# A flag mask taken through DRAM instead of a matrix product, three stores made whole, and another pace for the scans

## The chip, the cores and the metric

The kernel runs on one core of a Trainium2 chip. The metric is the device time of one execution in microseconds (us). The engines are called as the profile calls them: PE (matrix products; PEld is its weight load), DVE (vector), ACT (scalar), POOL (GpSimd) and SP, which here does little but issue DMA transfers.

## The reference

The input `x` is 2048 tokens of 448 channels, float32. Two branches read it, and a gate per token mixes them:

```python
g = sigmoid((x * gate_w).sum(-1, keepdims=True))
# a: a state-space layer: a kernel K of 256 complex exponentials per channel, convolved along the tokens
K = 2.0 * einsum("dn,dnl->dl", C, exp((A * dt) * pos)).real
a = causal_convolution(K, x) + x * D_skip
# b: an MLP mixer
h  = gelu(layernorm(x) @ w1)            # 448 -> 448
x1 = x + shifted_by_group(h) @ w2       # four channel groups moved by +1, -1, +2, -2 tokens
b  = x1 + gelu(layernorm(x1) @ w3) @ w4 # 448 -> 1792 -> 448
out = g * a + (1 - g) * b
```

## The kernel before

**Units.** The tokens are cut into four blocks of 512, each of four tiles of 128. PE works through 72 units: 16 small ones of kind "a" (layer w1/w2, four per block), then 14 of kind "d" for each block (128 of the 1792 hidden channels each). One unit is a run of products `first` (line 478, 11 matmuls of 512 columns for a "d" unit) into a bank `p`, and two units later a run `second` (line 602, 12 matmuls of 448 columns) that adds into four banks `acc`, one for each tile. Every float32 operand is split into a high and a low part, so that three products stand for one. Between the two, ACT makes the gelu `uf` (line 539) and its high part `uh` (line 549), and DVE the low part `ul` (line 569). At the end of a block, DVE takes the four `acc` banks into the result tile `xs` (`residual`, line 615); the next block's first `second` overwrites those banks, and so waits for it.

**The state-space branch.** For small rates the long convolution is the sum of four running sums. `ssm_guard` computes their coefficients `nuf`, and a flag for each partition, `rk[:, 4]`, which is 1 where the rates are small enough. `ssm_mask` makes one answer of the 128 flags, in every partition: `okm`. Where it holds, the coefficients are copied into `nu`, which had been zero; where it doesn't, a general convolution runs behind the kernel (`tc.If` in `gated_mix_kernel`, line 59 and 60), and each engine reads `okm` for that. The input of a step is loaded with 1 MB into `zs` (`ssm_load`), scaled on ACT by `nu` (`ssm_scale`, line 752), run through four scans on DVE (`ssm_scan`, line 757, a carry going by POOL), summed (`ssm_sum`), transposed (`ssm_turn`), sent through DRAM (`yd`, `ysb`) and added to the result (`ssm_out`, line 787). There are 16 such steps.

**Order.** Nothing is scheduled by a tool. Each engine carries out its instructions in the order in which the Python code issues them. The loop over units `n` calls what `at(n, ...)` has entered in the lists `before`, `after`, `between` and `late`; the scans' queue is paced by `ssm_some`, which gives it a credit of so many us of DVE work for each unit. SP's transfers stand in one queue in the same order, and a transfer that has to wait holds up those behind it.

**Transfers and their eight counters.** Each transfer counts on one of eight semaphores, handed out in turn (DMAHW0 to DMAHW7, called lanes here). At the end of the program SP waits for lane 0, lane 1 and so on to lane 7, one instruction each (line 60). A tile of the result goes out when both its branches have been added (`done`): whole, but in two halves of 64 rows for the first block.

Of the kernel before, what the change touches and what calls it, by code (L numbers as in the profile page):

```python
# [8 lines left out]
F32 = mybir.dt.float32  # L9
# [3 lines left out]
OP = mybir.AluOpType  # L13
AX = mybir.AxisListType
# [14 lines left out]
NF = F // 128  # L29
# [150 lines left out]
def mixer_and_small_steps(ctx, tc, xs, gg, okm, x, xT, xb, x0, w1, w2, w3, w4, gate, par, logdt, dskip, ident, out):  # L180
    nc = tc.nc

    big = ctx.enter_context(tc.tile_pool(name="big", bufs=1))
    wk = ctx.enter_context(tc.tile_pool(name="wk", bufs=2))
    ps = ctx.enter_context(tc.tile_pool(name="ps", bufs=2, space=PSUM))
    dr = ctx.enter_context(tc.tile_pool(name="dr", bufs=1, space=bass.MemoryType.DRAM))
# [19 lines left out]
    one = big.tile([128, 1], F32, name="one")  # L206
# [3 lines left out]
    rk = big.tile([128, 8], F32, name="rk")  # L210
# [244 lines left out]
    units = [("a", b, g) for b in range(NB) for g in (0, 2, 1, 3)] + \  # L455
# [5 lines left out]
    def first(n, bank="p1", seq=None, stop=True):  # L461

        kind, b, i = units[n]
        xh, xl = XH[kind, b], XL[kind, b]
        if kind == "a":
            wh, wl = (w1d, None) if i == 2 else (w1h[:, TI[i]], w1l[:, TI[i]])
            o = HALO - SHIFT[i]
        else:
            wh, wl = (w[:, :, i * 128:(i + 1) * 128] for w in (w3h, w3l))
            o = 0  # L470
        fresh = n not in P1
        if fresh:
            P1[n] = ps.tile([128, TB], F32, name="p1", tag=bank, bufs=3 if bank == "p1" else 1)
        p = P1[n]
        every = [(w, x_, k, 0, TB) for x_, ks in ((0, (0, 1, 2)), (0, (3,)), (1, (0, 1, 2))) for w in range(2 - x_)
                 for k in ks if not w or wl is not None]
        for q, (w, x_, k, t0, t1) in enumerate(seq or every):
            nc.tensor.matmul(p[:, t0:t1], (wl if w else wh)[:, k, :], (xl if x_ else xh)[:, k, o + t0:o + t1],  # L478
                             start=(q == 0 and fresh), stop=stop if q + 1 == len(seq or every) else False)
# [5 lines left out]
    def act_add(n, part=None):  # L485
        p = P1[n]
        if not part:
            UF[n] = wk.tile([128, TB], F32, name="uf")
            nc.scalar.activation(UF[n][:GD], p[GD:], AF.Copy)
        if part is not False:  # L490
            nc.vector.tensor_add(UF[n][:GD], p[:GD], UF[n][:GD])
# [63 lines left out]
    def act_head(n, later=False):  # L555
        drain(head_ops(n))
        if not later:
            drain(copy_ops(n))

    def act_copy(n):  # L560
        drain(copy_ops(n))

    def act_tail(n):
        kind, b, i = units[n]
        uf = UF.pop(n)
        if kind == "a" and i == 2:
            nc.vector.tensor_sub(UH[n][GD:], uf[:GD], f32(UH[n])[:GD])
        else:
            nc.vector.tensor_sub(UL[n], uf, f32(UH[n]))  # L569
# [3 lines left out]
    def done(b, j):  # L573
        q = NT * b + j
        parts[q] = parts.get(q, 0) + 1
        if parts[q] == 2:
            for p in range(0, 128, 64 if b == 0 else 128):
                t = slice(p, p + (64 if b == 0 else 128))
                nc.sync.dma_start(out[q * 128 + t.start:q * 128 + t.stop], xs[t, q, :])

    ADDED = {}
# [1 line left out]
    def second(n, only=None):  # L583
        kind, b, i = units[n]
        if kind == "a":
            wh, wl = w2h[:, i, :], w2l[:, i, :]
            s, e = i == 0, i == 3
        else:
            wh, wl = W4[i]
            s, e = i == 0, i == NF - 1  # L590
        q = [(j, p) for p in range(2 if kind == "a" and i == 2 else 3) for j in range(NT)]
        if s or e:
            q.sort()
        for j, p in only or q:
            first_, last_ = s and p == 0, (e or n == len(units) - 3 and j == NT - 1) and p == 2
            if only:
                ADDED[j] = ADDED.get(j, 0) + 1
                first_, last_ = ADDED[j] == 1, ADDED[j] == 11
            if first_:
                ACC[j] = ps.tile([128, D], F32, name=f"acc{j}", tag=f"acc{j}", bufs=1)  # L600
            t = slice(j * 128, (j + 1) * 128)
            nc.tensor.matmul(ACC[j], (UL if p == 2 else UH)[n][:, t], wl if p == 1 else wh,  # L602
                             start=first_, stop=last_)
        if e and not only:
            for j in range(NT):
                residual(n, j)

    def residual(n, j):
        kind, b, i = units[n]
        q = NT * b + j  # L610
        r = xs[:, q, :]
        if kind == "a":
            nc.vector.tensor_add(r, ACC[j], r)
        else:
            nc.vector.scalar_tensor_tensor(r, ACC[j], gs[:, q:q + 1], r, op0=OP.mult, op1=OP.add)
            done(b, j)
# [104 lines left out]
    def ssm_guard():  # L721
# [7 lines left out]
        nc.vector.tensor_scalar(rk[:, 0:4], rk[:, 0:4], RHO / L, None, op0=OP.is_le)  # L729
        nc.vector.tensor_reduce(rk[:, 4:5], rk[:, 0:4], axis=AX.X, op=OP.min)  # L730

    def ssm_mask():
        p = ps.tile([128, 1], F32, name="misc", bufs=1)
        nc.tensor.matmul(p, one.to_broadcast([128, 128]), rk[:, 4:5], start=True, stop=True)  # L734
        nc.vector.tensor_copy(rk[:, 5:6], p)
        nc.vector.tensor_scalar(okm, rk[:, 5:6].to_broadcast([128, 16]), 127.5, None, op0=OP.is_ge)
        nc.vector.copy_predicated(nu.rearrange("p a b -> p (a b)"), okm, nuf.rearrange("p a b -> p (a b)"))

    ZZ, ZS = {}, {}
# [66 lines left out]
    def ssm_some(n, amount):  # L806
        credit[0] += amount
        while queue and credit[0] > 0.0:
            cost, fn, a = queue.pop(0)
            credit[0] -= cost  # L810
            fn(*a)
            if fn is ssm_turn and a[1] == 3:
                for i in range(NT):
                    at(n + 1 + i // 2, ssm_back, a[0], i, when=late)
                    at(n + (2 if a[0] + 1 == NB else 3) + i // 2, ssm_out, a[0], i, when=late)
# [3 lines left out]
    before, between, after, late = {}, {}, {}, {}  # L819

    def at(n, fn, *a, when=after):
        when.setdefault(n, []).append((fn, a))

    def run(when, n):
        for fn, a in when.pop(n, []):
            fn(*a)
# [291 lines left out]
    def begin():  # L1118
        constants()
        first_loads()  # L1120
        nc.scalar.activation(rt, cm[:, 0:1], AF.Gelu_apprx_tanh)
        hl_tiles(("a", 0))
        hl_tiles(("a", 1))
        warm_up(7)
        for word in ORDER.split():
            name, _, codes = word.partition(":")
            if name[0] == "p" and codes:
                products(int(name[1]), codes)
            elif codes:
                second(int(name[1]), [(int(c[0]), int(c[1])) for c in codes.split(",")])  # L1130
            else:
                next(TASKS[name])
# [51 lines left out]
    for b in range(NB):  # L1184
        s0 = (7, 18, 31, 46)[b]
        for i in range(NT):
            n = s0 + (3, 4, 5, 3)[b] * (i // 2)
# [4 lines left out]
            q, when = n + (4 if b in (1, 2) else 3), late if b == 3 else before  # L1192
# [11 lines left out]
        for m in range(4):  # L1204
            at(q[m], ssm_moment, k, m)
    at(33, ssm_guard)
    at(34, ssm_mask, when=between)
    at(33, ssm_queue)
    for m in (3, 2, 1, 0):
        at(OWN, ssm_scale, 0, 0, m)  # L1210

# [2 lines left out]
    with tc.manual_schedule():  # L1214
        begin()
        for n in range(4, len(units)):
            if n >= 4 * NB - 2 and n + 1 < len(units):
                act_tail(n + 1)
            run(before, n)
            spent = sum(cost.get(fn, 0.0) for when in (after, late) for fn, _ in when.get(n, []))  # L1220
            run(after, n)
            if n < 4 * NB - 2 and n not in (7, 11):
                act_tail(n + 1)
            if n + LAG < len(units):
                first(n + LAG)
                if units[n + LAG][::2] == ("a", 2):
                    act_add(n + LAG, False)
            if n in (7, 11):
                second(n)
                act_tail(n + 1)  # L1230
            if n + LAG in UF:
                act_add(n + LAG, True)
            if n < OWN:
                run(between, n)
            if n + LAG < len(units) and n not in (6, 10):
                act_head(n + LAG, True)
            run(between, n)
            if n + LAG < len(units) and n not in (6, 10):
                act_copy(n + LAG)
            if n >= OWN:  # L1240
                ssm_some(n, 3.75 - (2.2 if units[n][2] == NF - 1 else 0.0) - spent)
            run(late, n)
            if n < len(units) - 2 and n not in (7, 11):
                second(n)
        last_two()
# [55 lines left out]
```

## Time and profile before

| what | before |
|---|---|
| median of 3 runs | 371.3 us (371.2 to 372.18) |
| the profiled execution | 371.42 us, span 369.6 us, granted clock 0.997 |
| PE busy | 363.9 us (98%) |
| DVE busy | 308.5 us (83%) |
| ACT busy | 216.1 us (58%) |
| POOL busy | 63.8 us (17%) |
| chain that ended last | PE 95%, DMA 3% |

The profiled execution took 371.42 us, of which 369.6 us lie between the first and the last instruction in the trace; a time worked out on the trace is set against 371.42, which is 0.1 us over the median. In the rows of the timeline the columns are: start in us, length in us, engine, line, operation, out<-in, count, and in brackets how long the engine stood idle before and what ended that.

### The profile page before, as it was taken

To read this page: it belongs to the slowest core of one execution; us is meant where nothing else is said; L and a number is where in the kernel's file an instruction comes from. 1 tells how busy PE (TensorE), PEld (TensorE's weight loads), DVE (VectorE), ACT (ScalarE), POOL (GpSimd) and SP (SyncE) were. 2 spreads that over 40 slices of the span, in tenths; PEclk is the share of its full clock that TensorE was granted. 3 is DMA by queue.
4 is the path that set the end of the run, shared out by engine and by line. 5 is a ranking of instruction groups with operands and counts; after the bars stand their busy time and mean duration, and the time that the engine had idled before them with its cause. 6 is when DMAs were issued, how large, how long until landed. Compare 5 with 4: busy or idle time off the path is not lost.

```text
span 369.6 us, 5310 instructions
## 1 busy us (share of the span) xinstructions
PE 363.9 (98%) x1734; PEld 314.8 (85%) x1734; DVE 308.5 (83%) x571; ACT 216.1 (58%) x383; POOL 63.8 (17%) x176
## 2 busy tenths in 40 slices
PE   8999999999999999999999999999999999999995
PEld 5988888888888888888888888888888888888884
DVE  4999979788989997388789899997889999999433
ACT  5887678776674737944373774554656745445220
POOL 1000433000400000110014333324234324000000
PEclk9999999999999999999999999999999999999998
DMA  7994116727938064001833514367485611361213
GB/s 268 394 398 143 48 54 128 160 82 254 381 122 192 2 121 150 0 0 51 192 93 82 84 28 121 86 178 126 86 127 114 177 27 25 72 178 30 66 48 105
DMA packets 88495, 46.14 MB, mean 125 GB/s; under 512 B 67216, under 2 KB 82960, under 8 KB 87824
## 3 DMA queue, kind: packets, MB, share of 16 engines
q1 hardware_dynamic: 88032, 45.27, 45.5%
q10 hardware_dynamic: 432, 0.49, 0.4%
q8 instruction: 15, 0.25, 0.3%
q14 instruction: 16, 0.13, 0.1%
HBM read 34.74 MB, written 11.01 MB: 124 GB/s over the span
## 4 chain that ended last, share of the span: by engine, by line
PE 95%; DMA 3%; SPq 0%; ACT 0%; DVE 0%; issue 0%
PE p L478 48%; PE acc L602 45%; DMA raw<-x_in 2%; DMA w1r<-w_in 1%; PE acc L637 1%; PE misc L363 0%; PE p L637 0%; SPq L246 0%; ACT xh L955 0%; SPq L264 0%; DVE xs L626 0%; PE misc L734 0%
## 5 line engine op out<-in xcount | busy, mean ns | idle before, releaser
L539 ACT ACTIVATE uf<-p 128x512 f32<-128x512 f32 x56 | 33.5, 599 | 113.3 <-PE p L478 113.3
L478 PE MATMUL p<-xh,w3l 128*128 128x512 f32 x224 | 70.1, 394 | 0.0
L478 PE MATMUL p<-xh,w3h 128*128 128x512 f32 x224 | 70.0, 394 | 0.0
L757 DVE TENSOR_TENSOR_SCAN z<-z,carry 128x512 f32<-128x512 f32 x48 | 61.6, 1283 | 4.2 <-POOL z L751 0.5
L602 PE MATMUL acc<-w4l,uh 128*128 128x448 f32 x216 | 56.3, 366 | 0.0
L602 PE MATMUL acc<-w4h,uh 128*128 128x448 f32 x216 | 56.0, 365 | 0.0
L602 PE MATMUL acc<-w4h,ul 128*128 128x448 f32 x216 | 55.8, 364 | 0.0
L569 DVE TENSOR_TENSOR ul<-uf,uh 128x512 fp32r<-128x512 f32 x56 | 38.1, 681 | 20.0 <-ACT uh L549 19.8
L478 PEld LDWEIGHTS p<-xh,w3l 128*128 128x128 f32 x224 | 42.1, 188 | 9.8
L478 PEld LDWEIGHTS p<-xh,w3h 128*128 128x128 f32 x224 | 42.1, 188 | 6.6
L478 PE MATMUL p<-xl,w3h 128*128 128x512 f32 x168 | 47.7, 392 | 0.0
L602 PEld LDWEIGHTS acc<-w4h,uh 128*128 128x128 f32 x216 | 40.5, 188 | 6.0
L602 PEld LDWEIGHTS acc<-w4h,ul 128*128 128x128 f32 x216 | 40.6, 188 | 3.6
L602 PEld LDWEIGHTS acc<-w4l,uh 128*128 128x128 f32 x216 | 40.5, 188 | 3.4
L752 ACT ACTIVATE z<-zs,nu 128x512 f32<-128x512 f32 x64 | 42.3, 710 | 0.2 <-DVE xl L409 0.2
L478 PEld LDWEIGHTS p<-xl,w3h 128*128 128x128 f32 x168 | 31.5, 188 | 7.2
L549 ACT ACTIVATE uh<-uf 128x512 fp32r<-128x512 f32 x56 | 35.4, 633 | 1.8
L751 POOL COPY z<-carry 128x1 f32<-128x1 f32 x48 | 32.7, 692 | 16.0 <-DVE zs L763 15.9
L759 POOL COPY carry<-z 128x1 f32<-128x1 f32 x48 | 13.1, 273 | 105.1 <-DVE z L757 104.4
L344 POOL TENSOR_TENSOR t<-r 128x4 f32<-128x4 f32 (+1 forms) x5 | 3.1, 626 | 117.4 <-DVE r L343 117.4
L757 DVE TENSOR_TENSOR_SCAN z<-z,carry,zero 128x512 f32<-128x512 f32 x16 | 20.0, 1248 | 0.0
L602 PE MATMUL acc<-w2l,uh 128*128 128x448 f32 x64 | 19.9, 367 | 0.0
(207 smaller groups left out, 543.7 us busy)
## 6 DMA issues: line engine op xcount, KB each, us to landing
zs<-xT_in SPq DMA_DIRECT2D x4, 1024.0 KB, 8.1
yd<-yt SPq DMA_DIRECT2D x56, 64.0 KB, 2.0
ysb<-yd SPq DMA_DIRECT2D x16, 224.0 KB, 2.7
raw<-xb_in SPq DMA_DIRECT2D x3, 1032.0 KB, 12.6
raw<-w_in SPq DMA_DIRECT2D x3, 1024.0 KB, 5.6
xd<-xt SPq DMA_DIRECT2D x16, 192.0 KB, 2.1
xr<-xd SPq DMA_DIRECT2D x16, 192.0 KB, 3.1
raw<-w_in SPq DMA_DIRECT2D x3, 896.0 KB, 4.6
```

Of the source, the lines that this page charges most:

```text
L344: eng.tensor_mul(t, y, y)
L478: nc.tensor.matmul(p[:, t0:t1], (wl if w else wh)[:, k, :], (xl if x_ else xh)[:, k, o + t0:o + t1], start=(q == 0 and fresh), stop=stop i ...
L539: nc.scalar.activation(UF[n], P1[n], AF.Gelu_apprx_tanh)
L549: nc.scalar.activation(UH[n], UF[n], AF.Copy)
L569: nc.vector.tensor_sub(UL[n], uf, f32(UH[n]))
L602: nc.tensor.matmul(ACC[j], (UL if p == 2 else UH)[n][:, t], wl if p == 1 else wh, start=first_, stop=last_)
L637: nc.tensor.matmul(acc, (UL if p == 2 else UH)[m][:, t], (wl if p == 1 else wh)[:, c], start=q == last and m == n and p == 0, stop=m > n a ...
L751: nc.gpsimd.tensor_copy(z4[:, m, 0:1], carry[:, k, m:m + 1])
L752: nc.scalar.activation(z4[:, m, 1:], ZS[b][:, k, :], AF.Copy, scale=nu[:, k, m:m + 1])
L757: nc.vector.tensor_tensor_scan(z, z, up, carry[:, k, m:m + 1], OP.add, OP.add)
L759: nc.gpsimd.tensor_copy(carry[:, k, m:m + 1], z[:, TB - 1:])
```

## The change

The flags no longer go through PE. `ssm_tell` writes the 128 flags to a row of DRAM, `ssm_hear` reads this row into all 128 partitions, and `ssm_mask` takes the minimum on DVE; it stands half a unit later in DVE's order. Of the first block's four tiles only tile 0 still goes out in halves. The scans' credit for a unit is 3.7 in place of 3.75 us.

```diff
     def done(b, j):
         ...
+        h = 64 if b == 0 and j < 1 else 128
         if parts[q] == 2:
-            for p in range(0, 128, 64 if b == 0 else 128):
-                t = slice(p, p + (64 if b == 0 else 128))
+            for p in range(0, 128, h):
+                t = slice(p, p + h)
                 nc.sync.dma_start(out[q * 128 + t.start:q * 128 + t.stop], xs[t, q, :])
...
+    def ssm_tell():
+        OKB.append(dr.tile([1, 128], F32, name="okd"))
+        nc.sync.dma_start(OKB[0].rearrange("o p -> p o"), rk[:, 4:5])
+
+    def ssm_hear():
+        OKB.append(big.tile([128, 128], F32, name="okb", tag="lt"))
+        row = OKB[0]
+        nc.sync.dma_start(OKB[1], bass.AP(tensor=row.tensor, offset=row.offset, ap=[[0, 128], [1, 128]]))
+
     def ssm_mask():
-        p = ps.tile([128, 1], F32, name="misc", bufs=1)
-        nc.tensor.matmul(p, one.to_broadcast([128, 128]), rk[:, 4:5], start=True, stop=True)
-        nc.vector.tensor_copy(rk[:, 5:6], p)
-        nc.vector.tensor_scalar(okm, rk[:, 5:6].to_broadcast([128, 16]), 127.5, None, op0=OP.is_ge)
+        nc.vector.tensor_reduce(rk[:, 5:6], OKB[1], axis=AX.X, op=OP.min)
+        nc.vector.tensor_scalar(okm, rk[:, 5:6].to_broadcast([128, 16]), 0.5, None, op0=OP.is_ge)
         nc.vector.copy_predicated(nu.rearrange("p a b -> p (a b)"), okm, nuf.rearrange("p a b -> p (a b)"))
...
     at(33, ssm_guard)
-    at(34, ssm_mask, when=between)
+    at(34, ssm_hear)
+    at(35, ssm_mask, when=before)
     at(33, ssm_queue)
+    at(33, ssm_tell)
...
-                ssm_some(n, 3.75 - (2.2 if units[n][2] == NF - 1 else 0.0) - spent)
+                ssm_some(n, 3.7 - (2.2 if units[n][2] == NF - 1 else 0.0) - spent)
```

On PE one matmul goes (it runs as two passes) and nothing else moves. On DVE, around units 34 and 35, stands before (`ul` is the low part that PE waits for, `xl` and `xh` the split input of the next block, the `BN` pair its statistics, `z` the scans):

```order
L303 BN_AGGR st<-b_1981 128x2 x2
L735 COPY rk<-misc 128x1
L736 TENSOR_SCALAR okm<-rk 128x16
L737 COPY_PREDICATED nu<-okm,nuf 128x16
L569 TENSOR_TENSOR ul<-uf,uh 128x512
L409 TENSOR_TENSOR xl<-xr,xh 128x3x128
L410 TENSOR_TENSOR xh<-xr,xh 64x128
L409 TENSOR_TENSOR xl<-xr,xh 128x3x128
L410 TENSOR_TENSOR xh<-xr,xh 64x128
L301 BN_STATS b_2029<-xs 128x6 x2
```

The three instructions of the mask stand ahead of five of the block's own. On DVE at the same place stands now:

```order
L303 BN_AGGR st<-b_1983 128x2 x2
L569 TENSOR_TENSOR ul<-uf,uh 128x512
L409 TENSOR_TENSOR xl<-xr,xh 128x3x128
L410 TENSOR_TENSOR xh<-xr,xh 64x128
L409 TENSOR_TENSOR xl<-xr,xh 128x3x128
L410 TENSOR_TENSOR xh<-xr,xh 64x128
L746 TENSOR_REDUCE rk<-okb 128x1
L747 TENSOR_SCALAR okm<-rk 128x16
L748 COPY_PREDICATED nu<-okm,nuf 128x16
L301 BN_STATS b_2031<-xs 128x6 x2
```

The mask has moved behind those five, it begins with the minimum over `okb`, and everything from the statistics on is queued behind it. On SP, at the place where the scans' input is loaded, stands now:

```order
L755 DMA zs<-xT_in 128x4x512 x2
L738 DMA okd<-rk 128x1
L743 DMA okb<-okd 128x128
L59 TENSOR_LOAD okm
L59 ISA x2
L432 DMA xd<-xt 128x3x128
L434 DMA xd<-xt 128x64
```

The two new transfers stand directly behind the two loads of 1 MB; before, the read of `okm` (line 59) followed those loads at once. At the end of DVE's list, where `xs<-ysb` is the last of the state-space branch and the rows with `acc` the last residuals, stood before:

```order
L569 TENSOR_TENSOR ul<-uf,uh 128x512 x2
L787 SCALAR_TENSOR_TENSOR xs<-ysb,gg,xs 128x448 x2
L569 TENSOR_TENSOR ul<-uf,uh 128x512
L787 SCALAR_TENSOR_TENSOR xs<-ysb,gg,xs 128x448 x2
L569 TENSOR_TENSOR ul<-uf,uh 128x512
L626 SCALAR_TENSOR_TENSOR xs<-acc_3181,gs,xs 128x448
```

and now, by the other pace:

```order
L569 TENSOR_TENSOR ul<-uf,uh 128x512 x2
L798 SCALAR_TENSOR_TENSOR xs<-ysb,gg,xs 128x448 x2
L569 TENSOR_TENSOR ul<-uf,uh 128x512
L798 SCALAR_TENSOR_TENSOR xs<-ysb,gg,xs 128x448 x2
L627 SCALAR_TENSOR_TENSOR xs<-acc_3175,gs,xs 128x448
```

The last four additions of the state-space branch come one unit later, the last two of them directly ahead of the last residuals. SP issues 214 transfers in the program before and 213 now (two more, three fewer), so the last store counts on lane 7, where before it counted on lane 0.

More of the change, by code (lines that the diff above doesn't have):

```diff
@@ L730, in ssm_guard @@
         nc.vector.tensor_reduce(rk[:, 4:5], rk[:, 0:4], axis=AX.X, op=OP.min)
+    OKB = []
+    def ssm_tell():
[5 more added lines that the diff above has]
+        nc.sync.dma_start(OKB[1], bass.AP(tensor=row.tensor, offset=row.offset, ap=[[0, 128], [1, 128]]))
     def ssm_mask():
-        p = ps.tile([128, 1], F32, name="misc", bufs=1)
-        nc.tensor.matmul(p, one.to_broadcast([128, 128]), rk[:, 4:5], start=True, stop=True)
-        nc.vector.tensor_copy(rk[:, 5:6], p)
-        nc.vector.tensor_scalar(okm, rk[:, 5:6].to_broadcast([128, 16]), 127.5, None, op0=OP.is_ge)
+        nc.vector.tensor_reduce(rk[:, 5:6], OKB[1], axis=AX.X, op=OP.min)
+        nc.vector.tensor_scalar(okm, rk[:, 5:6].to_broadcast([128, 16]), 0.5, None, op0=OP.is_ge)
         nc.vector.copy_predicated(nu.rearrange("p a b -> p (a b)"), okm, nuf.rearrange("p a b -> p (a b)"))
```

## The prediction

> **What bounds the kernel now.** The profile's page comes first: the busy shares, and the shares of the chain that ended last.
>
> ```profile
> PE 363.9 (98%) x1734; PEld 314.8 (85%) x1734; DVE 308.5 (83%) x571; ACT 216.1 (58%) x383; POOL 63.8 (17%) x176
> PE 95%; DMA 3%; SPq 0%; ACT 0%; DVE 0%; issue 0%
> ```
>
> PE is busy without a break, so only what PE executes, what makes PE wait, and what stands behind PE's last product can move the end. A faster DVE or a shorter transfer gains nothing by itself. The chain of waits around the mask, in order of time (start, length, what), shows the product that goes:
>
> ```profile
> 177.79 2.43 PE acc L602 x12
> 180.22 2.55 PE p L478 x11
> 182.77 0.12 PE misc L734 x2
> 182.89 2.55 PE acc L602 x12
> 185.44 2.56 PE p L478 x11
> 188.01 2.43 PE acc L602 x12
> ```
>
> A unit is 2.55 + 2.43 = 4.98 us. The one with the flags' product takes 185.44 - 180.22 = 5.22 us: 0.12 for the product, and 0.12 because the run behind it takes 2.55 in place of 2.43. At the other end stand the instructions of line 60, in which SP waits for the eight lanes, and the last two stores:
>
> ```profile
> L60 SPq EVENT_SEMAPHORE  x8: 17/17/17, 367.7 to 368.2; - x8
> L643 SPq DMA_DIRECT2D out_dram<-xs x2: 348/386/423, 365.0 to 365.5; - x2
> DMA to landing us min/median/max: 2.2/2.3/2.4
> ```
>
> The last store is issued at 365.5 and lands 2.2 us later, at 367.7: just when the first of the eight waits ends. It counts on lane 0, so the other seven waits, long fulfilled, are gone through after it, in 0.5 us.
>
> **What goes, step by step.** The product: 0.24 us of PE's time, all of it on the path. The eight waits: with the last store on lane 7, seven of them are past before it lands, and 0.5 us go. Three stores made whole: three issues fewer on SP, in the middle of the kernel and with nobody waiting for the stores; they only shift the lane, and cost nothing. Together this is 0.74 us.
>
> **What comes: the way of the flags.** These rows are the timeline's row for the flags on DVE, the two loads of `zs` (issue, and time to landing), and the page's rows on transfers.
>
> ```profile
> 179.15 0.16 DVE L730 TENSOR_REDUCE rk<-rk 128x1 f32<-128x4 f32 x1
> L744 SPq DMA_DIRECT2D zs<-xT_in x2: 613/622/632, 178.5 to 179.1; - x2
> DMA to landing us min/median/max: 6.7/8.3/9.8
> L659 SPq DMA_DIRECT2D gr<-gate_in x1: 2851/2851/2851, 13.8 to 13.8; - x1
> L1047 SPq DMA_DIRECT2D dsk<-dskip_in x1: 522/522/522, 16.7 to 16.7; - x1
> L1048 SPq DMA_DIRECT2D dts<-logdt_in x1: 518/518/518, 17.3 to 17.3; - x1
> gr<-gate_in SPq DMA_DIRECT2D x1, 224.0 KB, 14.2
> dsk<-dskip_in SPq DMA_DIRECT2D x1, 2.0 KB, 11.5
> dts<-logdt_in SPq DMA_DIRECT2D x1, 2.0 KB, 11.1
> yd<-yt SPq DMA_DIRECT2D x56, 64.0 KB, 2.0
> xr<-xd SPq DMA_DIRECT2D x32, 32.0 KB, 2.6
> ```
>
> The flags are ready at 179.3. SP has issued the second load of `zs` by 179.1 + 0.6 = 179.7 and then sends the flags. But 2 MB are ahead of them. That a small transfer waits for large ones ahead of it is shown by `dsk` and `dts`: 2 KB each, issued at 16.7 and 17.3, landing at 28.2 and 28.4, right behind `gr` ahead of them (13.8 + 14.2 = 28.0); some 0.2 us for each. The second `zs` lands at 179.1 + 9.8 = 188.9, hence the flags in DRAM at 189.1. Only then may SP issue the way back. For its 64 KB the nearest rows are 2.0 (the same bytes) and 2.6 us (smaller pieces, read back from DRAM like these); I take 2.2, nearer to the row of the same size, and land at 189.2 + 2.2 = **191.4**, between 191.2 and 191.8 by these rows.
>
> The Trainium skill, page "DMA: Bandwidth & Descriptors", section "Anatomy of one DMA — SWDGE (gpsimd) path", gives about 2.0 us as the fixed cost of one transfer, plus its bytes at 436 GB/s. By it alone two hops end near 184, and the sum would be 370.7. The `dts` row speaks against taking it alone; the same page of the Trainium skill, section "Queues, rings and completion order", says that each DMA engine takes descriptors in ring order, and by that rule, too, the flags come behind the 2 MB; the rows agree with their 11.1 us.
>
> **What DVE does meanwhile.** DVE's timeline:
>
> ```profile
> 183.33 0.18 DVE L737 COPY_PREDICATED nu<-okm,nuf 128x16 f32<-128x16 int32 x1
> 186.21 0.29 DVE L410 TENSOR_TENSOR xh<-xr,xh 64x128 fp32r<-64x128 f32 x1
> 186.53 1.15 DVE L301 BATCH_NORM_STATS2 b<-xs 128x6 f32<-128x448 f32 x2
> 192.17 0.67 DVE L569 TENSOR_TENSOR ul<-uf,uh 128x512 fp32r<-128x512 f32 x1
> 209.26 0.70 DVE L569 TENSOR_TENSOR ul<-uf,uh 128x512 fp32r<-128x512 f32 x1 [0.16 <-ACT uh L549]
> 211.01 0.56 DVE L409 TENSOR_TENSOR xl<-xr,xh 128x384 fp32r<-128x384 f32 x1 [1.04 <-ACT xh L448]
> 226.50 1.28 DVE L757 TENSOR_TENSOR_SCAN z<-z,carry 128x512 f32<-128x512 f32 x1
> 228.49 2.52 DVE L615 SCALAR_TENSOR_TENSOR xs<-acc,gs,xs 128x448 f32<-128x448 f32 x4 [0.70 <-PE acc L602]
> L706 DVE TENSOR_REDUCE mom<-pk x4: 405/412/415, 106.6 to 171.4; 128x1 f32<-128x256 f32 x4
> ```
>
> In the new order DVE reaches the mask at 186.5 and stands until 191.4. The minimum over 128 columns costs some 0.3 us (0.41 for 256 columns), compare and select 0.2 each as now: the statistics start at 192.1 in place of 186.53, **5.6 us late**. Queued behind the mask on DVE are the scans and every `ul` that PE needs; on ACT the first four `ssm_scale` wait for `nu`, with the next `uf` and `uh` behind them; on SP the read of `okm`, and behind it `xd`, which waits for DVE anyway.
>
> Two deadlines of PE follow, from PE's and PEld's timelines:
>
> ```profile
> 199.44 0.36 PE L602 MATMUL acc<-w4h,ul 128*128 128x448 f32 x1
> 232.43 0.19 PEld L602 LDWEIGHTS acc<-w4h,uh 128*128 128x128 f32 x1
> ```
>
> The first: the `ul` that ended at 192.84 would end at 198.4; its product stands at 199.44, less the 0.24 gained and 0.2 for the weights ahead of it: 199.0. Covered, with 0.6 us left; without that cover each further us would be a us of PE. ACT's four scalings, 2.6 us from 192.1, and `uf` and `uh`, 1.3, end near 196, also in time.
>
> The second decides. Between 192 and 228 DVE has almost no idle time to catch up with: 0.16 + 1.04 us. So 5.6 - 1.2 = 4.4 us are left when it comes to the residuals of the block's end. Now DVE is free for them at 226.50 + 1.28 = 227.78; then at 232.2, and the first of the four (2.52/4 = 0.63, with its end 0.68) is through at 232.9. PE's first product into that bank loads its weights at 232.43, or 232.2 with the 0.24 gained. PE **waits 0.7 us**. The three residuals behind it take 0.63 each, PE's three products for each tile about as much, so nothing is added. Bounds from the rows of the way back: 0.5 to 1.1 us.
>
> After that DVE has idle time again and its lateness wears off; and 3.7 us of scan credit lighten each later unit by 0.05. That is costed at nothing on PE, since PE waits for no scan now. Its price is at the end: two additions more stand ahead of the last residuals there.
>
> ```profile
> 354.38 1.27 DVE L787 SCALAR_TENSOR_TENSOR xs<-ysb,gg,xs 128x448 f32<-128x448 f32 x2
> 358.75 0.69 DVE L569 TENSOR_TENSOR ul<-uf,uh 128x512 fp32r<-128x512 f32 x1 [3.10 <-ACT uh L549]
> 361.13 0.69 DVE L626 SCALAR_TENSOR_TENSOR xs<-acc,gs,xs 128x448 f32<-128x448 f32 x1 [0.55 <-PE acc L637]
> ```
>
> They run from 359.4 to 360.7, and the residual that started at 359.90 starts 0.8 us late; but each one behind it has 0.55 us of idle time ahead, so by the third the lateness is gone. Cost: nothing, 0.8 us if that idle time weren't there.
>
> **Sum.** 371.42 - 0.24 - 0.5 + 0.7 = 371.4 on the profiled execution, which is 0.1 us over the median of the runs: **371.3 us**. A measurement of this kernel can tell about 0.3%, 1.1 us, from no change, so this is no change.
>
> **Rivals.** *The flags come early* (they overtake the loads, or these run faster): by the 2.0 and 2.2 us of the rows they would be back at 184, before DVE gets to the mask at 186.5; any landing before 190.7 leaves PE without a wait. 370.7, or a little under with the median. For it: nothing but the small size; against it the `dts` row. The page "DMA: Bandwidth & Descriptors" of the Trainium skill, section "Queues, rings and completion order", adds that completion is not in order of issue for one issuing engine, which leaves this open; no row here shows it.
>
> *The flags come later, and the kernel is slower.* The place is the same two deadlines; the price is one us for each us of landing after 190.7, and from 192.5 on it is over the 1.1 us. The length of the `zs` transfers isn't steady. Two lone loads of 1 MB, issued at 225.7 and at 270.7, landed after:
>
> ```profile
> DMA to landing us min/median/max: 6.5/6.5/6.5
> DMA to landing us min/median/max: 9.6/9.6/9.6
> ```
>
> With 3.1 us more on `zs` the sum is 374.5; with half of it, 372.9. A longer write of 128 single values, or more idle time lost on DVE than counted, acts in the same way. I expect 373 in this case.
>
> *The lane gains nothing*, because SP's barrier behind the waits is held by another engine: 0.5 us more, 371.8, still no change. All other engines have ended by 366, so I give it no chance of its own.
>
> **Chances.** The forecast 0.52, early flags 0.20, late flags 0.28. The forecast lies within 0.3% whole (370.5 to 372.3); early flags mostly too, and under 370.2 (0.10) only where the lighter pace or the shorter queue of stores gains something more that I have costed at nothing; late flags over 372.4. So faster 0.10, same 0.62, slower 0.28. The range is 370.4 to 373.1: from the early case to half of the late one.
>
> **What would show it.** The mask's row on DVE with an idle time of about 5 us ended by a DMA; SP waiting some 9 us for `okd`; PE idle 0.5 to 1.1 us at 232, in the row of line 603 that waits for the residual; no product in the chain at 182.8; the eight waits at the end with seven of them over before the store lands. Wrong would be: a landing of `okb` before 190.7 or after 192.5, or a wait of PE at another place.

## The result, and the profile after

| | before | after |
|---|---|---|
| median of the runs | 371.74 us | 376.84 us |
| profiled execution, its span | 371.42, 369.6 us | 376.38, 374.6 us |
| mean granted TensorE clock | 0.997 | 0.993 |

The ratio is 1.0139 (95% interval 1.012 to 1.0157): the kernel is 5 us slower. One of the six executions of `half`, an experiment below, took 930.48 us, for a reason that stays open, and is left out of its figures. The page of the changed kernel shows where to look: PE's busy time, the shares of the chain, and the one group of PE's products that waited (busy and mean, then idle time and what ended it).

```profile
PE 365.1 (97%) x1732; PEld 315.1 (84%) x1732; DVE 307.4 (82%) x571; ACT 215.9 (58%) x383; POOL 65.9 (18%) x176
PE 88%; DMA 6%; ACT 2%; DVE 2%; issue 0%; SPq 0%; ACTq 0%
L603 PE MATMUL acc<-w4h,uh 128*128 128x448 f32 x216 | 56.8, 369 | 3.8 <-ACT uh L549 3.8
```

PE has two products fewer and is 1.2 us longer busy, and it stood still for 3.8 us, once. The chain, 95% PE's before, now runs 6% over transfers. Followed in time, it shows where the flags were late (start, length, what):

```profile
180.26 13.72 DMA okd<-rk
194.00 0.03 issue
194.03 3.47 DMA okb<-okd
197.53 0.30 DVE rk L746
```

The flags land at 194.0 in place of the 189.1 that I forecast, and are back at 197.5 in place of 191.4. The transfers of that stretch with their median time from issue to landing, and the packets that moved between 188.6 and 194:

```profile
zs<-xT_in SPq DMA_DIRECT2D x2, 1024.0 KB, 8.0
okb<-okd SPq DMA_DIRECT2D x1, 64.0 KB, 3.5
okd<-rk SPq DMA_DIRECT2D x1, 0.5 KB, 13.7
DMA packets 0, 0.00 MB, mean 0 GB/s; under 512 B 0, under 2 KB 0, under 8 KB 0
```

The loads of `zs` behave as before; the second has landed at 188.9. From 188.6 on not one packet moves, and still the flags' write isn't done for 5.4 us. The trace keeps 16 reports of `okd`, as many as the core has DMA engines, each with its moment (us):

```
188.51 188.64 188.68 189.81 190.05 190.22 190.38 191.20
191.49 191.79 192.44 192.60 193.04 193.19 193.64 193.98
```

The flags' packets end within 0.1 us of the loads' last one, at 188.6; the reports trickle in until 193.98. What follows on ACT and PE, from their timelines (idle time and its end in brackets), and PE's granted clock (fourth column: busy time with its count, then PEclk):

```profile
198.27 2.56 ACT L763 ACTIVATE z<-zs,nu 128x512 f32<-128x512 f32 x4 [12.63 <-DVE nu L748]
201.34 0.63 ACT L549 ACTIVATE uh<-uf 128x512 fp32r<-128x512 f32 x1
197.40 0.85 PE L478 MATMUL p<-xl,w3h 128*128 128x512 f32 x3
202.02 1.86 PE L603 MATMUL acc<-w4h,uh 128*128 128x448 f32 x4 [3.77 <-ACT uh L549]
197.00:202.00 5.00, 1.25 (x6) 0.99 0.02 3
202.00:205.00 3.00, 2.98 (x8) 0.50 0.00 0
205.00:208.00 3.00, 3.00 (x15) 0.95 0.03 5
```

Behind the mask ACT makes four scalings, then `uf` and `uh`; PE has its `uh` 4.5 us after the landing, and needed it at 198.25. After the wait the clock is granted at half: in 202 to 205 PE gets through 8 products in the time of 15. The end of the program, answering to the rows of line 60 of before:

```profile
L60 SPq EVENT_SEMAPHORE  x8: 17/17/17, 372.2 to 373.2; - x8
L644 SPq DMA_DIRECT2D out_dram<-xs x2: 333/366/398, 370.8 to 371.2; - x2
```

The last store lands at 373.19, and the last of the eight waits starts at 373.21, with no other behind it. The span ends 1.41 us after the landing; before it was 1.95.

### The profile page after: what moved, and what is told of

Its sections match the earlier page's. It is cut to its first block, busy times and chain, and to the rows that moved or that the text cites. A ratio compares the mean times of both kernels' runs of the same rounds, so it can differ in the third digit from the quotient of the medians.

```text
span 374.6 us, 5305 instructions
## 1 busy us (share of the span) xinstructions
PE 365.1 (97%) x1732; PEld 315.1 (84%) x1732; DVE 307.4 (82%) x571; ACT 215.9 (58%) x383; POOL 65.9 (18%) x176
## 4 chain that ended last, share of the span: by engine, by line
PE 88%; DMA 6%; ACT 2%; DVE 2%; issue 0%; SPq 0%; ACTq 0%
PE p L478 44%; PE acc L603 42%; DMA okd<-rk 4%; DMA raw<-x_in 2%; PE acc L638 1%; DMA okb<-okd 1%; ACT z L763 1%; PE pm L877 1%; PE p L638 0%; DVE mw L712 0%; ACT uh L549 0%; PE misc L363 0%; DVE ul L569 0%; ACT uf L539 0%; DVE mw L714 0%
## 5 line engine op out<-in xcount | busy, mean ns | idle before, releaser
L603 PE MATMUL acc<-w4h,uh 128*128 128x448 f32 x216 | 56.8, 369 | 3.8 <-ACT uh L549 3.8
L762 POOL COPY z<-carry 128x1 f32<-128x1 f32 x48 | 33.9, 717 | 14.8 <-DVE zs L774 14.7
## 6 DMA issues: line engine op xcount, KB each, us to landing
xd<-xt SPq DMA_DIRECT2D x16, 192.0 KB, 2.1
xr<-xd SPq DMA_DIRECT2D x16, 192.0 KB, 3.1
```

The source lines that it names most:

```text
L762: nc.gpsimd.tensor_copy(z4[:, m, 0:1], carry[:, k, m:m + 1])
```

## The experiments

**The flags in four pieces (`rows`).** Two rivals for the late write: its single values, or its place behind 2 MB.

```
-        OKB.append(dr.tile([1, 128], F32, name="okd"))
-        nc.sync.dma_start(OKB[0].rearrange("o p -> p o"), rk[:, 4:5])
+        OKB.append(dr.tile([4, 32], F32, name="okd"))
+        s, t = (big.tile([128, 32], F32, name=n, tag=n) for n in ("oks", "okt"))
+        nc.vector.tensor_copy(s, rk[:, 4:5].to_broadcast([128, 32]))
+        nc.vector.transpose(t, s)
+        nc.sync.dma_start(OKB[0], t[0:128:32, :])
```

> The flags are turned on DVE (a 32x32 transpose of the column) and go to DRAM as four pieces of 32 values each instead of 128 single values; place in the queue, read back, stores and pace as in the changed kernel. Theory A (single values): the 128 pieces of 4 bytes were what made the write late, 5.1 us behind the second load of zs; four pieces should land within 0.5 us of that load, about 189.3, the read back 3.5 us later at 193, and the time falls by some 4.5 us to 372.3. Rival B (place in the queue): any small write behind 2 MB of loads is acknowledged 5 us after them; then okd still lands near 194 and the time stays at 376.8.

Measured: 370.96 us against 371.89 of before, ratio 0.9963 (0.995 to 0.9976). SP's row for the read back, which is issued when the write has landed, the mask on DVE, and PE's weight load for the first product that waits for a residual of block 1's end:

```profile
L746 SPq DMA_DIRECT2D okb<-okd x1: 340/340/340, 189.2 to 189.2; - x1
192.03 0.29 DVE L749 TENSOR_REDUCE rk<-okb 128x1 f32<-128x128 f32 x1 [5.17 <-DMA okb<-okd]
232.03 1.25 DVE L616 SCALAR_TENSOR_TENSOR xs<-acc,gs,xs 128x448 f32<-128x448 f32 x2
232.80 0.19 PEld L603 LDWEIGHTS acc<-w4h,uh 128*128 128x128 f32 x1 [0.31 <-issue]
```

The same 512 bytes behind the same 2 MB land by 189.2, together with the last of them, as the prediction had it for the single values; and the time is 5.9 us under that of the changed kernel. It is 1.3 us under my number, too: the read back landed at 192.0, not 193, and the deadline is later than I had it (below). So the place in the queue costs what I said, and the single values cost the rest; what about them is dear, the probes below tell.

**The write ahead of the loads (`first`).** The mirror image: single values, but ahead of the loads.

```
-    at(33, ssm_queue)
     at(33, ssm_tell)
+    at(33, ssm_queue)
```

> The write of the flags is issued ahead of the two loads of zs, single values as in the changed kernel; the read back stays behind the loads. Theory A (single values): the write needs about 2 + 5 us also in an empty queue and lands near 186.5; the loads start 1.2 us later and end near 190; the read back, issued at 186.5 and behind what is left of them, lands near 193.5: 372.5 to 373. Rival B (place): the write lands 2 us after its issue, near 182, and the read back, issued then, lands right behind the loads, near 191: 371.5.

Measured: 377.23 us, 1.0126 (1.0104 to 1.0147): no better than the changed kernel. The write, the read back, and PE's wait:

```profile
okd<-rk SPq DMA_DIRECT2D x1, 0.5 KB, 7.8
okb<-okd SPq DMA_DIRECT2D x1, 64.0 KB, 9.5
201.50 1.86 PE L603 MATMUL acc<-w4h,uh 128*128 128x448 f32 x4 [3.51 <-ACT uh L549]
```

With the loads behind it the write still takes 7.8 us, so theory A holds here too. My number was 4 us too low: the read back fell behind the loads (9.5 us, landing at 197.0, not 193.5), and PE's granted clock fell to half, which is priced below.

**The lane and the pace by themselves (`lane`, `pace`).**

```
+        h = 64 if b == 0 and j < 3 else 128          (lane)
-            for p in range(0, 128, 64 if b == 0 else 128):
-                t = slice(p, p + (64 if b == 0 else 128))
+            for p in range(0, 128, h):
+                t = slice(p, p + h)
...
-                ssm_some(n, 3.75 - (2.2 if ...       (pace)
+                ssm_some(n, 3.7 - (2.2 if ...
```

> The kernel before, mask by the product and pace 3.75 as there, with one of the first block's four tiles stored whole: one store fewer, so that the last store counts on lane 7. The prediction's step: seven of the eight waits at the end are over before the store lands, 0.5 us less: 371.2 where the kernel before has 371.7, the span ending 1.4 us after the last landing in place of 1.9. Rival: the barrier behind the waits is held by another engine, no change.

> The kernel before with scans paced at 3.7 in place of 3.75, nothing else. The prediction's step: no change (371.7, within 0.3). Rival: the lighter pace moves scans across a unit and costs or gains over 0.5 us; a cost of that size would explain part of the lost 5 us.

Measured: `lane` 371.13 us, 0.9974 (0.9964 to 0.9983), `pace` 371.81 us, 0.9998 (0.9986 to 1.001). In `lane` the span ends 1.41 us after the last landing where before has 1.95: 0.54 us, the forecast step. The pace alone changes nothing. Neither holds any part of the loss.

**What a write of single values costs (`probe`, `probe2`).** Extra transfers in the kernel before, for which nobody waits.

```
+    at(n, probe, i, when=late)      # n = 39, 41, 49, 56, 58, 60, one transfer at each
+    # probe, writes: the flags' column rk[:, 4:5] to a DRAM tile [128, step], column 0
+    # probe, reads:  ident_in, one row for all partitions (pe); its 128 rows (pf)
```

> The kernel before with six extra transfers at quiet places, for which nothing waits: the column of 128 flags (a) into one row of 512 bytes, (b) each flag into a row of its own of 512 bytes, (c) each into its own 64 bytes, (d) 64 flags into one row of 256 bytes; then reads of (e) one row of 512 bytes for all 128 partitions and (f) 128 different rows. Theory A1 (one place): writes of 4 bytes that fall in one row are taken one after the other, about 43 ns each; (a) lands 7 us after its issue, (d) 4.5 us, (b) and (c) about 2 us. Rival A2 (each small write costs by itself): (b) and (c) take 7 us as well. For the read back: if one row read 128 times is the cost, (e) takes about 3 us and (f) 2 us; if not, both about 2.

> The kernel before with six extra writes to DRAM at the same quiet places, nobody waiting: 16 single values into 64 bytes (a), 32 into 128 bytes (b), 128 values 8 bytes apart (c), 16 apart (d), 32 apart (e), and 128 pieces of 8 bytes side by side (f). Measured so far, from issue to landing: 128 values side by side 7.4 us, 64 side by side 6.2, 128 values 64 or 512 bytes apart 1.6 to 1.7. Theory L (writes into the same 64 bytes wait for each other, some 0.3 us each, and different 64 bytes go on beside each other): the time follows the writes that share 64 bytes: (a) and (b), 16 of them, about 6 us; (c) and (f), 8 of them, about 4; (d), 4, about 3; (e), 2, about 2. Rival S (all of a transfer's writes of 4 bytes in one neighbourhood go one by one, 43 ns each): (a) 2.4, (b) 3, (c), (d) and (f) about 7.

The last column is the time to landing; each is one transfer in one execution (371.66 and 371.35 us in all). First `probe`: (a) 128 values side by side, (b) 512 bytes apart, (c) 64 bytes apart, (d) 64 side by side, (e) one row read 128 times, (f) 128 rows read.

```profile
pa<-rk SPq DMA_DIRECT2D x1, 0.5 KB, 7.4
pb<-rk SPq DMA_DIRECT2D x1, 0.5 KB, 1.7
pc<-rk SPq DMA_DIRECT2D x1, 0.5 KB, 1.6
pd<-rk SPq DMA_DIRECT2D x1, 0.2 KB, 6.2
pe<-ident_in SPq DMA_DIRECT2D x1, 64.0 KB, 3.2
pf<-ident_in SPq DMA_DIRECT2D x1, 64.0 KB, 2.9
```

Then `probe2`: (a) 16 values side by side, (b) 32, (c) 128 values 8 bytes apart, (d) 16, (e) 32 bytes apart, (f) 128 pieces of 8 bytes side by side.

```profile
pa<-rk SPq DMA_DIRECT2D x1, 0.1 KB, 1.6
pb<-rk SPq DMA_DIRECT2D x1, 0.1 KB, 3.6
pc<-rk SPq DMA_DIRECT2D x1, 0.5 KB, 2.9
pd<-rk SPq DMA_DIRECT2D x1, 0.5 KB, 2.5
pe<-rk SPq DMA_DIRECT2D x1, 0.5 KB, 1.7
pf<-rk SPq DMA_DIRECT2D x1, 1.0 KB, 4.4
```

128 writes of 4 bytes land after 1.6 to 1.7 us where they lie 32 bytes apart or more. Side by side they take 7.4 us. So it is neither the count nor the size of the pieces (A2 falls), but that they are neighbours (A1); A1's even 43 ns a value doesn't hold, for 64 values took 6.2 us where it wanted 4.5. The finer theory L falls too: 16 values in the same 64 bytes cost nothing (1.6 us, where L wanted 6), and S, one by one at 43 ns, wanted 7 for 8 bytes' distance and got 2.9. Close together, 32 pieces are dear and 16 are not. The distance of their starts isn't all: (c) and (f) of `probe2` both start every 8 bytes, and the longer pieces of (f) take 4.4 us against 2.9. Why 16 are free stays open: it may be their number, or that with 16 reports for a transfer each engine has one piece only, which no run here separates. Which unit of memory the pieces wait for stays open, too.

The Trainium skill, page "DMA: Bandwidth & Descriptors", section "Specifications", says that transfers under 512 bytes are done by reading, changing and writing back. That would fit neighbours that wait for each other, which no run here shows; taken by size alone it would make (b) and (c) of `probe` as dear as (a), and the runs speak against that.

The read back is not settled: one row read by all takes 3.2 us, but 128 rows 2.9, with an issue of 1.47 us in place of 0.45.

**How the landing becomes time (`half`, `most`).** By mixing single values with pieces of 32, the landing is moved. The prediction had named two deadlines, behind ACT and DVE's residuals; these runs tell which decides.

```
# half: as rows, but for the last line; most: with 3 and 96 in place of 2 and 64
-        nc.sync.dma_start(OKB[0], t[0:128:32, :])
+        nc.sync.dma_start(OKB[0][2:], t[64:128:32, :])
+        nc.sync.dma_start(OKB[0][:2].rearrange("(o a) p -> (a p) o", o=1), rk[:64, 4:5])
...
-        h = 64 if b == 0 and j < 1 else 128
+        h = 128
```

> As the changed kernel, but 64 of the 128 flags go as two pieces of 32 values, and 64 as single values (one transfer more on SP; the first block's stores are all whole, so the last store keeps lane 7). By 43 ns a value the write lands near 191.4 and the read back near 194.4. Theory D (VectorE's lateness decides): every us of landing after 191.9 is paid once, at the residuals of block 1's end: 371.0 + 2.5 = 373.5. Rival P (ScalarE's scalings decide): PE only waits for uh, from a landing of 193.7 on, and the clock drops only if that wait lasts over 3.4 us: 371.0 + 0.7 = 371.7, clock undisturbed.

> The same with 96 single values and one piece of 32. The write lands near 192.7, the read back near 195.8. Theory D: 371.0 + 3.9 = 374.9. Rival P: a wait of 2.1 us for uh and no drop of the clock, 373.1; with a drop of 3.4 us to half the clock, 374.8, and then the window of half clock must show in the profile.

Measured: `half` 375.2 us, 1.0081 (1.0059 to 1.0103); `most` 378.98 us, 1.0177 (1.0154 to 1.0199). Both landings missed my numbers, at 196.4 and 199.6: the loads of `zs` ended later (189.2 and 190.2), the write isn't linear in its values (3.3 and 4.6 us behind them for 64 and 96 values), and the read back took 3.8 and 4.7 us. Read by the landings that happened, `half` tells the theories apart: D wants 371.0 + 4.5 = 375.5, P 371.0 + 2.7 = 373.7. First `half` (mask, PE's waits, the residual, PEclk behind the first wait), then `most`:

```profile
196.45 0.29 DVE L750 TENSOR_REDUCE rk<-okb 128x1 f32<-128x128 f32 x1 [9.52 <-DMA okb<-okd]
200.95 1.08 PE L603 MATMUL acc<-w4h,uh 128*128 128x448 f32 x4 [2.80 <-ACT uh L549]
203.08 1.08 PE L603 MATMUL acc<-w4h,ul 128*128 128x448 f32 x4 [0.22 <-DVE ul L569]
236.48 2.43 DVE L616 SCALAR_TENSOR_TENSOR xs<-acc,gs,xs 128x448 f32<-128x448 f32 x4
237.28 0.45 PE L603 MATMUL acc<-w4h,uh 128*128 128x448 f32 x1 [0.69 <-ACT uf L539]
202.00:205.00 3.00, 2.78 (x14) 1.00 0.02 5
```

```profile
199.62 0.29 DVE L750 TENSOR_REDUCE rk<-okb 128x1 f32<-128x128 f32 x1 [11.98 <-DMA okb<-okd]
204.11 1.86 PE L603 MATMUL acc<-w4h,uh 128*128 128x448 f32 x4 [5.25 <-ACT uh L549]
```

In `half` PE waits three times: 2.8 us for `uh`, with the clock left at 1.00, briefly at 203.1 for DVE's `ul`, and again at 237.3. The row names ACT's `uf` for the last, but what ends just ahead is the first residual, started on DVE at 236.48, 0.6 us long. How late the same product of PE stands against the kernel before, at five places (us of before), with the landing of the flags ahead and the stretch of half clock in the trace's record behind:

```
         landing   182.2   187.1   200.7   235.6   355.2   half clock
lane        -      +0.25   +0.25   +0.25   +0.25   +0.25   none
rows1     187.5    +0.43   +0.19   +0.17   +0.17   +0.17   none
rows      192.0    +0.36   +0.12   +0.10   +0.26   +0.25   none
half      196.4    +0.44   +0.20   +3.76   +4.71   +4.70   none
first     197.0    +0.28   +0.04   +6.29   +6.40   +6.40   200.39, 6.83 us long
after     197.5    +0.54   +0.29   +5.81   +5.78   +5.77   201.87, 3.41 us long
most      199.6    +1.15   +0.91   +8.89   +8.90   +8.90   202.73, 6.83 us long
```

The first column is the start of the program, different in each execution, and not the change's. Between it and the second the product goes: -0.24 in every kernel that sends the flags by DRAM. `rows` just touches the residuals' deadline (+0.16 at 235.6), so it stands at a landing of about 191.9; `half` landed 4.4 us later and lost 4.5 in all. With each program's start (column 187.1) taken out, it landed 4.35 us behind `rows` and lost 4.4 us more. D is right for it: 1 us for each us. Of the 4.5 us, 3.6 had gone already in the first two waits; the residual brought it to the full sum.

Where PE stood 3.5 us or more in one wait, theory P with the clock comes to a sum as large as D's or larger; D is taken here with each program's start taken out. In `first`: 3.51 of waiting, and of the 6.83 us of half clock 1.11 lie in the wait, so (6.83 - 1.11) / 2 = 2.86, together 6.4; lost 6.4, while D would give 5.2. In `most`: 5.25 + (6.83 - 1.38) / 2 = 8.0; lost 8.0, while D would give 7.0. In the changed kernel the two come to the same: 3.77 + (3.41 - 0.15) / 2 = 5.4, and D 5.5. PE got to the residuals as they were ready, which is why its lag doesn't grow there. That it would have waited there without the clock's loss is read from this, not tried.

Why one stretch of half clock is 3.41 us long and another 6.83 can be read from the records of the clock. In each trace its changes, over the whole span, lie whole multiples of 3.413 us apart, so they mark the borders of windows. In `first` these are 196.98, 200.39, 203.80 and 207.22, and PE stood from 197.99 to 201.50:

```profile
197.00:202.00 5.00, 1.49 (x6) 0.84 0.01 2
202.00:207.00 5.00, 5.00 (x15) 0.50 0.01 3
```

So the clock fell 2.40 us into the wait, behind a window in which PE had still worked for 1.01 us. It came back behind the first window without a pause of PE; the one before it held the last 1.11 us of the wait. The others agree. In the changed kernel PE stood through one whole window, and for 0.15 us of the next, behind which the clock was back; in `most` through one and for 1.38 us of the next, and the half clock lasted for one window more; in `half` the wait of 2.80 us fell 1.00 and 1.80 us into two windows, and the clock stayed. As far as these four traces show, what counts is how much of one window PE stands; the limit for the fall would lie between 1.80 and 2.40 us.

**The version with nothing left to wait for (`rows1`).** The four pieces of `rows`, and the second load of `zs` behind the read back.

```
-        ssm_load(0)
-        ssm_load(1)
+        ssm_load(0)
...
     at(34, ssm_hear)
+    at(34, ssm_load, 1)
```

> The four pieces of 32 flags, and the second load of zs issued behind the read back. The write is behind 1 MB only and should land near 185.5, the read back near 188.5, before any deadline. PE then waits nowhere: 370.9, or 0.1 less than with the four pieces alone (370.96), where the read back landed at 192.0, 0.1 us too late for the residuals. A landing after 191.9, or a time over 371.5 with an early landing, would speak against the deadline read from the traces.

Measured: 371.15 us, 0.9977 (0.9962 to 0.9991). The flags are back at 187.5 and PE waits nowhere, as the table shows. It can't be told from `rows` (0.9963) or `lane` (0.9974): all three are 0.2 to 0.4% faster than before, and 5 to 6 us faster than the change as made.

## Why the prediction was wrong

- **The product off PE, -0.24:** right, in every run that has it.
- **The lane, -0.5:** right, 0.54.
- **Three stores whole, pace 3.7, nothing:** right for the pace; the stores' number mattered through the lane alone in `lane`. The other two weren't run apart, but `rows` has all three stores as changed and is no slower than `lane`.
- **"0.2 us for each" behind the loads: this step failed.** The queue was judged rightly: the flags' packets left right behind the second load, by 188.6. But I read the landing of a write from `dsk` and `dts`, which are loads, in rows of 16 bytes for each partition, into SBUF. For 128 single values written side by side to DRAM the page of before had no row, and the one condition that matters, neighbouring pieces, wasn't seen. 5.1 us behind the load in place of 0.2: +4.9.
- **The way back, 2.2 us:** 3.5 here, 2.8 to 4.7 in the others (9.5 in `first`, behind the loads): +1.3, outside my bounds of 2.0 to 2.6. Together the landing was 6.1 us late, 197.5 for 191.4.
- **The deadlines:** right as places, wrong in which one decides here. The prediction let ACT's path be in time and put PE's wait at the residuals, at 232. In the changed kernel PE waited for `uh` at 198.25, on ACT's path, which is in time only up to a landing of about 193.8 (4.5 us from landing to `uh`), and came to the residuals without a wait. The residuals' deadline was off in size, too: 191.9 in `rows`, or about 191.5 with its later start (+0.36) taken out, and not 190.7. DVE made up 1.9 us by then (6.12 us late behind the mask, 4.25 at the residual), not 1.2. A landing at the forecast 191.4 would have been just in time. In the kernel before DVE had 0.48 us more of idle time, at 190.97, which the sum from 192 on left out:

```profile
190.97 1.28 DVE L757 TENSOR_TENSOR_SCAN z<-z,carry 128x512 f32<-128x512 f32 x1 [0.48 <-POOL z L751]
```

- **The price of 1 us for each us:** right where the clock holds (`half`), too low in `first` and `most`, where PE stood 3.51 and 5.25 us in one wait. The half clock was no term of the prediction; in the changed kernel it holds 1.6 of the 5.4 us.
- **The terms as they came:** with the 5.5 us that the changed kernel lost (5.77 - 0.29 in the table), 371.42 - 0.24 - 0.54 + 5.5 = 376.1; the profiled execution took 376.38.
- **The rival with late flags** named what came, even the longer write of single values; its 373 was 4 us short, because it was priced by the spread of the loads and not by a bound of its own for the write. From its own rule the 197.5 that came gives 370.7 + 6.8 = 377.5. That this is close to 376.8 is luck in part: its deadline was too early, and the time went in another wait and in the clock.

## What to carry to other kernels

Don't hand a column of 128 values to another engine or partition through DRAM as single values side by side: turn it first, so that it goes in a few long pieces. Values laid 32 bytes apart were as quick in a probe, but weren't tried in the kernel. A price read from loads was none for this write; where the page has no row for a transfer's direction and shape, the upper bound has to be wide, or a lone probe in a quiet stretch gives it in one run. And look at how long PE would stand in one go: waits of 3.51 and 3.77 us cost 6.4 and 5.4 us here, while a wait of 2.80 us left the clock alone.

## What the runs showed of the hardware

- 128 writes of 4 bytes to DRAM: 7.4 to 7.8 us from issue to landing side by side, 1.6 to 1.7 us from 32 bytes' distance on; 16 side by side 1.6, 32 3.6, 64 6.2. All packets can be gone while the write is unconfirmed for 5 us more.
- The granted clock after a wait of PE: 1.00 after 2.80 us, half for 3.41 us after 3.77, half for 6.83 us after 3.51 and after 5.25. The Trainium skill, page "TensorE: Matmul & The Clock Gate", section "Part 1: The HAM clock gate", says that the clock goes to half after an idle window of about 3.4 us, counted in free-running windows of 3.41 us. The traces agree on the windows: all changes of the clock lie whole multiples of 3.413 us apart. They differ on the idle window: in `first` the clock fell behind one in which PE stood for 2.40 us only, and it stayed up in `half` behind one with 1.80 us. It came back behind a window with 0.15 us of standing or none, and not behind those with 1.11 and 1.38 us.
